# Sketched attention and a feed-forward block on one core: attention of the next batch placed among the feed-forward steps by a list scheduler, query sketches repeated by DMA

## Chip, core and metric

The kernel runs on one core of a Trainium2 chip. The metric is the device time of one execution in microseconds (us), as the median of several. The profiler's "span" is a little shorter than that time (by 1.75 us in the profiled run of the changed kernel). An execution is called slow when it is over 1.5% above the fastest one of the same kernel. Medians below are of all executions of a run; ratios and differences use the fast ones.

In profile lines, PE is TensorE's matmul work, PEld its weight loads, DVE is VectorE, ACT is ScalarE, POOL is GpSimd. SPq is the queue of SyncE, which issues most DMAs. L235 means line 235 of that kernel's own file, so the same line number in two kernels is not the same statement.

## The reference

There are 4 batches, 4 heads, 1088 tokens and a head size of 32. Each query and key is projected with two small 8x32 matrices. The products of the two sketches form 64 features, and attention becomes two small products with a division per token and head. The result (4352 tokens of 128) goes through a feed-forward block with a squared ReLU.

```python
def _attn_ref(q, k, v, S1, S2):              # q, k, v: (4, 4, 1088, 32); S1, S2: (8, 32)
    def phi(x):
        a = np.einsum('rd,bhsd->bhsr', S1, x)
        b = np.einsum('rd,bhsd->bhsr', S2, x)
        return np.einsum('bhsi,bhsj->bhsij', a, b).reshape(*x.shape[:-1], r * r)
    q_p, k_p = (phi(q), phi(k))
    kv = np.einsum('bhsf,bhsd->bhfd', k_p, v)
    z = np.sum(k_p, axis=2)
    num = np.einsum('bhsf,bhfd->bhsd', q_p, kv)
    den = np.einsum('bhsf,bhf->bhs', q_p, z)[..., None] + 1e-06
    return (num / den).astype(np.float32)

def _moe_ref(x, w_in, w_out):                # (4352, 128), (128, 2048), (2048, 128)
    h = x @ w_in
    r = np.maximum(h, 0.0)
    g = r * r
    return (g @ w_out).astype(np.float32)
```

The features of all queries need each sketch number next to each of eight others, so something has to repeat them. And a batch's feed-forward work needs only that batch's attention, so attention of a later batch can run beside it.

## The kernel before

Attention of all four batches comes first. The numerator is computed with the 32 outputs of a head on partitions and tokens along the free dimension, so the denominator of 512 tokens is one row on a single partition:

```python
            for hh in range(G):
                ...
                    nc.tensor.matmul(nd_ps[:, :C], kvz_sb[:, hh, :], qpT_all[:, hh, c0 : c0 + C],
                                     start=True, stop=True)
                    rec = den_pool.tile([1, NDC], F32, tag="rec")
                    nc.vector.reciprocal(rec[:, :C], nd_ps[D : D + 1, :C])          # L235
                    recb = den_pool.tile([D, NDC], F32, tag="recb")
                    nc.gpsimd.partition_broadcast(recb[:, :C], rec[:, :C])
                    nc.vector.tensor_mul(xT[h * D : (h + 1) * D, ...], nd_ps[:D, :C], recb[:, :C])
```

Then the feed-forward stage takes 512 tokens at a time, in 16 steps of 128 hidden units, two steps in flight:

```python
            for ct in range(C_TILES):
                hT = hT_psum_pool.tile([128, R_TILE], F32, tag="hT")
                nc.tensor.matmul(hT[:, :R], w_in_sb[:, ct, :], xT[:, r0 : r0 + R], start=True, stop=True)
                tmp = tmp_pool.tile([128, R_TILE], BF16, tag="tmp")
                nc.scalar.activation(tmp[:, :R], hT[:, :R], mybir.ActivationFunctionType.Relu)   # L270
                gT = gT_pool.tile([128, R_TILE], BF16, tag="gT")
                nc.vector.tensor_mul(gT[:, :R], tmp[:, :R], tmp[:, :R])                          # L274
                op = out_ps0 if ct % 2 == 0 else out_ps1
                nc.tensor.matmul(op[:, :R], w_out_sb[:, ct, :], gT[:, :R], ...)
```

The whole kernel:

Of the kernel before, what the change touches and what calls it, by code (L numbers as in the profile page):

```python
# [10 lines left out]
F32 = mybir.dt.float32  # L12
F32R = mybir.dt.float32r
BF16 = mybir.dt.bfloat16


def _mk_p2(nc, pool, a_sb, b_rep, P, r, F, tag, eng=None):
    p_out = pool.tile([128, 2 * F], F32, tag=tag, name=tag)
    (eng or nc.vector).tensor_tensor(  # L19
        out=p_out[:P].rearrange("p (hh i j) -> p hh i j", hh=2, i=r),  # L20
        in0=a_sb[:P, :, None].rearrange("p (hh i) j -> p hh i j", hh=2).to_broadcast(
            [P, 2, r, r]
        ),
        in1=b_rep[:P].rearrange("p (hh i j) -> p hh i j", hh=2, i=r),
        op=mybir.AluOpType.mult,
    )
    return p_out


def _mk_p(nc, pool, a_sb, b_rep, P, r, F, tag):  # L30
    p_out = pool.tile([128, F], F32, tag=tag, name=tag)
    nc.vector.tensor_tensor(
        out=p_out[:P].rearrange("p (i j) -> p i j", i=r),
        in0=a_sb[:P, :, None].to_broadcast([P, r, r]),
        in1=b_rep[:P].rearrange("p (i j) -> p i j", i=r),
        op=mybir.AluOpType.mult,
    )
    return p_out
# [3 lines left out]
def kernel(  # L42
# [11 lines left out]
    nc = tc.nc  # L54
    B, H, S, D = q.shape
    r = S1.shape[0]
    F = r * r
    d_model = moe_w_in.shape[0]
    d_ff = moe_w_in.shape[1]
    N_TOK = B * S  # L60
    assert d_model == H * D
    C_TILES = d_ff // 128
    G = 128 // D
    n_stiles = (S + 127) // 128

    consts = ctx.enter_context(tc.tile_pool(name="consts", bufs=1))

    S1Tf = consts.tile([D, r], F32)
    S2Tf = consts.tile([D, r], F32)
    nc.sync.dma_start(out=S1Tf, in_=S1.rearrange("r d -> d r"))  # L70
    nc.sync.dma_start(out=S2Tf, in_=S2.rearrange("r d -> d r"))
    S12Eb = consts.tile([128, G * r + G * F], F32)
    nc.gpsimd.memset(S12Eb, 0.0)
    for g in range(G):
        nc.vector.tensor_copy(
            S12Eb[g * D : (g + 1) * D, g * r : (g + 1) * r], S1Tf
        )
        nc.vector.tensor_copy(
            out=S12Eb[
                g * D : (g + 1) * D, G * r + g * F : G * r + (g + 1) * F  # L80
            ].rearrange("d (i j) -> d i j", i=r),
            in_=S2Tf[:, None, :].to_broadcast([D, r, r]),
        )

    ident = consts.tile([128, 128], F32)
    make_identity(nc, ident)
    xT = consts.tile([d_model, N_TOK], BF16)

    w_in_sb = consts.tile([128, C_TILES, 128], BF16)
    nc.gpsimd.dma_start(  # L90
        out=w_in_sb, in_=moe_w_in.rearrange("d (ct c) -> d ct c", c=128)
    )
    w_out_sb = consts.tile([128, C_TILES, 128], BF16)
    nc.gpsimd.dma_start(
        out=w_out_sb, in_=moe_w_out.rearrange("(ct c) d -> c ct d", c=128)
    )

    with (
        tc.tile_pool(name="qkT", bufs=2) as qkT_pool,
        tc.tile_pool(name="qkin", bufs=3) as qkin_pool,  # L100
        tc.tile_pool(name="vp", bufs=2) as v_pool,
        tc.tile_pool(name="proj", bufs=3) as proj_pool,
        tc.tile_pool(name="kp", bufs=3) as kp_pool,
        tc.tile_pool(name="qpT", bufs=2) as qpT_pool,
        tc.tile_pool(name="kvzsb", bufs=2) as kvz_pool,
        tc.tile_pool(name="den", bufs=3) as den_pool,
        tc.tile_pool(name="ps_a", bufs=2, space=bass.MemoryType.PSUM) as ps_a,
        tc.tile_pool(name="ps_t", bufs=2, space=bass.MemoryType.PSUM) as ps_t,
        tc.tile_pool(name="ps_kvz", bufs=2, space=bass.MemoryType.PSUM) as ps_kvz,
        tc.tile_pool(name="ps_nd", bufs=2, space=bass.MemoryType.PSUM) as ps_nd,  # L110
    ):
        bh = [(b, h) for b in range(B) for h in range(H)]
        for g in range(len(bh) // G):
            heads = bh[g * G : (g + 1) * G]
            b0 = heads[0][0]
            assert all(bb == b0 for bb, _ in heads)
            h0 = heads[0][1]

            qab_all_a = qkT_pool.tile([128, n_stiles, G * r], F32, tag="qab_a")
            qab_all_b = qkT_pool.tile([128, n_stiles, G * F], F32, tag="qab_b")  # L120
            kvz_ps = ps_kvz.tile([128, G * (D + 1)], F32, tag="kvz")
            for ti in range(n_stiles):
                s0 = ti * 128
                P = min(128, S - s0)
                q4 = qkin_pool.tile([128, 128], F32, tag="q4")
                k4 = qkin_pool.tile([128, 128], F32, tag="k4")
                nc.sync.dma_start(
                    out=q4[:P].rearrange("p (g d) -> p g d", d=D),
                    in_=q[b0, h0 : h0 + G, s0 : s0 + P, :].rearrange(
                        "g p d -> p g d"  # L130
                    ),
# [192 lines left out]
```

## Time and profile before

| | before |
|---|---|
| time, median of 3 | 368.46 us (368.08 to 369.57) |
| span of the profile | 366.2 us |
| attention ends, feed-forward starts | about 280 us |

The first lines of the profile page of the kernel before give busy time per engine, then the busy share in tenths in 40 equal slices of the span. PEclk is TensorE's granted clock in tenths of full speed. The last line shown is the chain of waits that ended last, split by line of code:

```profile
...
PE 262.6 (72%) x848; PEld 116.2 (32%) x850; DVE 272.6 (74%) x543; ACT 131.6 (36%) x386; POOL 38.7 (11%) x93
...
DVE  1146878995597899558879964898997888888874
...
PEclk9999555556965555596555559955555999999998
...
DVE rec L235 30%; PE nd_ps L227 9%; ACT tmp L270 6%; PE qab_ps L144 5%; PE kvz_ps L180 5%; PE kab_ps L164 5%; DVE gT L274 4%; PE hT L262 3%; POOL recb L237 3%; DVE xT L238 3%; PE qpT_ps L214 3%; DVE qpT_all L216 2%; PE qT_ps L140 2%; DVE qp
...
```

VectorE is busy 74% and TensorE 72%, but neither is the bound everywhere. The chain of waits shows the one-row reciprocal first, with 30% of the span. The clock row shows half speed through most of attention.

The groups of instructions by shape (count, busy us, mean ns of one, idle before and its causes):

```profile
...
L235 DVE RECIPROCAL rec<-nd_ps 1x512 f32<-1x512 f32 x32 | 105.5, 3324 | 12.4 <-PE nd_ps L227 12.4
L274 DVE TENSOR_TENSOR gT<-tmp 128x512 bf16<-128x512 bf16 x128 | 53.6, 422 | 15.5 <-ACT tmp L270 12.0 <-PE out_ps_2114 L276 0.3 <-PE out_ps_2577 L276 0.3
...
L235 DVE RECIPROCAL rec<-nd_ps 1x64 f32<-1x64 f32 x16 | 8.8, 549 | 0.5
...
```

```profile
...
L270 ACT ACTIVATE tmp<-hT 128x512 bf16<-128x512 f32 x128 | 72.4, 598 | 36.9 <-DVE gT L274 32.0 <-PE hT L262 1.6 <-PE ot_ps L290 1.1
...
```

A reciprocal of 512 numbers on one partition takes 3324 ns, 114 us for all 48. With 64 elements it takes 549 ns, so its cost follows the elements along the free dimension, and 127 partitions do nothing. A square of a full 128x512 tile costs 422 ns.

Busy time of each engine by stretch: two stretches of attention, and 9 us of the feed-forward stage:

```profile
...
100.00:200.00 100.00, 67.45 (x179) 30.29 (x180) 79.85 (x133) 17.89 (x84) 13.39 (x29) 0.58 0.13 21
245.00:280.00 35.00, 18.85 (x33) 3.67 (x33) 31.25 (x31) 3.79 (x7) 7.08 (x11) 0.50 0.00 0
300.00:309.00 9.00, 8.71 (x34) 3.19 (x33) 7.49 (x20) 8.72 (x16) 0.00 (x0) 1.00 0.07 22
...
```

Columns after the stretch: its length, busy us of PE, PEld, DVE, ACT, POOL, then granted clock, DMA share and GB/s. In attention the clock is 0.58 and 0.50. In the feed-forward stage ScalarE is full (8.72 of 9 us), at clock 1.00. TensorE's 8.71 us is as high, but the ends of matmuls are modelled in the profile, so this is no sign that it is at its peak.

### The profile page before, as it was taken

To read this page: it belongs to the slowest core of one execution; us is meant where nothing else is said; L and a number is where in the kernel's file an instruction comes from. 1 tells how busy PE (TensorE), PEld (TensorE's weight loads), DVE (VectorE), ACT (ScalarE), POOL (GpSimd) and SP (SyncE) were. 2 spreads that over 40 slices of the span, in tenths; PEclk is the share of its full clock that TensorE was granted. 3 is DMA by queue.
4 is the path that set the end of the run, shared out by engine and by line. 5 is a ranking of instruction groups with operands and counts; after the bars stand their busy time and mean duration, and the time that the engine had idled before them with its cause. 6 is when DMAs were issued, how large, how long until landed. Compare 5 with 4: busy or idle time off the path is not lost.

```text
span 366.2 us, 3606 instructions
## 1 busy us (share of the span) xinstructions
PE 262.6 (72%) x848; PEld 116.2 (32%) x850; DVE 272.6 (74%) x543; ACT 131.6 (36%) x386; POOL 38.7 (11%) x93
## 2 busy tenths in 40 slices
PE   0698365786836688593678659476654999999995
PEld 0474122335512233461223246221111333333332
DVE  1146878995597899558879964898997888888874
ACT  1144110001421100142110014241112999999984
POOL 1200011111001112101102210001211000000000
PEclk9999555556965555596555559955555999999998
DMA  7864001102400101150020122000000100100001
GB/s 108 86 100 64 2 15 21 20 10 35 78 7 13 24 12 16 29 85 7 0 34 9 19 32 35 0 0 0 0 0 2 30 30 29 30 23 21 18 26 44
DMA packets 61620, 10.19 MB, mean 28 GB/s; under 512 B 57120, under 2 KB 61472, under 8 KB 61600
## 3 DMA queue, kind: packets, MB, share of 16 engines
q1 hardware_dynamic: 59392, 8.92, 14.2%
q0 software_dynamic: 2208, 1.05, 2.3%
q8 instruction: 7, 0.11, 0.1%
q14 instruction: 13, 0.11, 0.1%
HBM read 8.78 MB, written 2.23 MB: 30 GB/s over the span
## 4 chain that ended last, share of the span: by engine, by line
DVE 42%; PE 37%; ACT 9%; issue 5%; POOL 3%; POOLq 0%; ACTq 0%; DVEq 0%
DVE rec L235 30%; PE nd_ps L227 9%; ACT tmp L270 6%; PE qab_ps L144 5%; PE kvz_ps L180 5%; PE kab_ps L164 5%; DVE gT L274 4%; PE hT L262 3%; POOL recb L237 3%; DVE xT L238 3%; PE qpT_ps L214 3%; DVE qpT_all L216 2%; PE qT_ps L140 2%; DVE qp L19 1%; DVE osb L292 1%
## 5 line engine op out<-in xcount | busy, mean ns | idle before, releaser
L235 DVE RECIPROCAL rec<-nd_ps 1x512 f32<-1x512 f32 (+1 forms) x48 | 114.3, 2399 | 12.9 <-PE nd_ps L227 12.4
L270 ACT ACTIVATE tmp<-hT 128x512 bf16<-128x512 f32 (+1 forms) x144 | 77.8, 574 | 38.4 <-DVE gT L274 32.8
L227 PE MATMUL nd_ps<-qpT_all,kvz_sb 64*33 64x512 f32 (+1 forms) x96 | 62.3, 773 | 40.2 <-DVE xT L238 39.5
L274 DVE TENSOR_TENSOR gT<-tmp 128x512 bf16<-128x512 bf16 (+1 forms) x144 | 57.8, 408 | 16.8 <-ACT tmp L270 13.2
L262 PE MATMUL hT<-xT,w_in_sb 128*128 128x512 bf16 (+1 forms) x143 | 54.5, 389 | 2.3 <-ACT tmp L270 0.6
L237 POOL PARTITION_BROADCAST recb<-rec x48 | 31.9, 664 | 152.8 <-DVE rec L235 152.8
L168 ACT COPY ka_sb<-kab_ps 128x32 f32<-128x32 f32 (+1 forms) x36 | 6.7, 185 | 104.7 <-PE kab_ps L164 104.7
L214 PE MATMUL qpT_ps<-ident,qp 128*128 128x128 f32 (+1 forms) x72 | 22.4, 368 | 24.4 <-DVE qp L19 17.3
L19 DVE TENSOR_TENSOR kp<-ka_sb,kab_ps 128x128 f32<-128x128 f32 (+1 forms) x72 | 18.2, 283 | 23.7 <-ACT ka_sb L168 23.0
L180 PE MATMUL kvz_ps<-vpad,kp 128*128 128x66 f32 (+1 forms) x144 | 28.1, 323 | 7.2 <-issue 6.2
L144 PE MATMUL qab_ps<-S12Eb,qT_sb 128*128 128x288 f32 (+1 forms) x72 | 32.8, 548 | 0.4
L164 PE MATMUL kab_ps<-S12Eb,kT_sb 128*128 128x288 f32 (+1 forms) x72 | 32.6, 543 | 0.0
L227 PEld LDWEIGHTS nd_ps<-qpT_all,kvz_sb 64*33 64x33 f32 x96 | 10.3, 143 | 70.1 <-issue 57.3
L180 PEld LDWEIGHTS kvz_ps<-vpad,kp 128*128 128x128 f32 (+1 forms) x144 | 23.6, 230 | 21.4 <-issue 19.3
L215 ACT COPY qpT_all<-qpT_ps 64x128 f32<-64x128 f32 (+1 forms) x72 | 16.2, 254 | 39.2 <-PE qpT_ps L214 38.7
L238 DVE TENSOR_TENSOR xT<-nd_ps,recb 32x512 bf16<-32x512 f32 (+1 forms) x48 | 24.9, 525 | 7.1 <-POOL recb L237 6.5
L19 DVE TENSOR_TENSOR qp<-qab_all_a,qab_all_b 128x128 f32<-128x128 f32 (+1 forms) x72 | 20.5, 299 | 9.7 <-ACT qab_all_b L148 5.0
L214 PEld LDWEIGHTS qpT_ps<-ident,qp 128*128 128x128 f32 (+1 forms) x72 | 10.3, 163 | 46.4 <-issue 30.7
L262 PEld LDWEIGHTS <-w_in_sb 128*128 128x128 bf16 x144 | 14.2, 100 | 29.6 <-issue 24.3
L276 PEld LDWEIGHTS <-w_out_sb 128*128 128x128 bf16 x144 | 13.8, 98 | 26.4 <-issue 15.8
L216 DVE COPY qpT_all<-qpT_ps 64x128 f32<-64x128 f32 (+1 forms) x72 | 18.6, 283 | 2.6 <-ACT qpT_all L215 1.9
L152 DVE COPY kT_sb<-kT_ps 128x128 f32<-128x128 f32 (+1 forms) x36 | 10.1, 280 | 13.6 <-PE kT_ps L150 13.4
(202 smaller groups left out, 199.0 us busy)
## 6 DMA issues: line engine op xcount, KB each, us to landing
out_dram<-osb SPq DMA_DIRECT2D x34, 64.0 KB, 1.6
vpad<-in_v_dram SPq DMA_DIRECT2D x32, 64.0 KB, 2.3
w_in_sb<-in_moe_w_in_dram POOLq DMA_DIRECT2D x1, 512.0 KB, 5.6
w_out_sb<-in_moe_w_out_dram POOLq DMA_DIRECT2D x1, 512.0 KB, 7.8
vpad<-in_v_dram SPq DMA_DIRECT2D x4, 32.0 KB, 2.2
q_121<-in_q_dram SPq DMA_DIRECT2D x1, 64.0 KB, 5.6
k_122<-in_k_dram SPq DMA_DIRECT2D x1, 64.0 KB, 5.4
q_150<-in_q_dram SPq DMA_DIRECT2D x1, 64.0 KB, 5.2
```

Of the source, the lines that this page charges most:

```text
L19: (eng or nc.vector).tensor_tensor(out=p_out[:P].rearrange("p (hh i j) -> p hh i j", hh=2, i=r), in0=a_sb[:P, :, None].rearrange("p (hh i) ...
L144: nc.tensor.matmul(qab_ps[:P], qT_sb[:, :P], S12Eb, start=True, stop=True)
L164: nc.tensor.matmul(kab_ps[:P], kT_sb[:, :P], S12Eb, start=True, stop=True)
L180: nc.tensor.matmul(kvz_ps[:, hh * (D + 1) : (hh + 2) * (D + 1)], kp[:P, :], vpad[:P, hh : hh + 2, :].rearrange("p g d -> p (g d)"), start= ...
L214: nc.tensor.transpose(qpT_ps[:, :P], qp[:P], ident[:P, :P])
L227: nc.tensor.matmul(nd_ps[:, :C], kvz_sb[:, hh, :], qpT_all[:, hh, c0 : c0 + C], start=True, stop=True,)
L235: nc.vector.reciprocal(rec[:, :C], nd_ps[D : D + 1, :C])
L237: nc.gpsimd.partition_broadcast(recb[:, :C], rec[:, :C])
L238: nc.vector.tensor_mul(xT[h * D : (h + 1) * D, b0 * S + c0 : b0 * S + c0 + C], nd_ps[:D, :C], recb[:, :C],)
L262: nc.tensor.matmul(hT[:, :R], w_in_sb[:, ct, :], xT[:, r0 : r0 + R], start=True, stop=True,)
L270: nc.scalar.activation(tmp[:, :R], hT[:, :R], mybir.ActivationFunctionType.Relu)
L274: nc.vector.tensor_mul(gT[:, :R], tmp[:, :R], tmp[:, :R])
```

## The change

The kernel is rebuilt. Its intent is to have no one-partition work, fewer and larger instructions, and attention of batches 1 to 3 hidden among the 68 feed-forward steps.

1. Tokens lie on partitions in the numerator, so a reciprocal works on 128x12.
2. A feed-forward step is 1024 columns wide, and its ReLU can run on ScalarE or VectorE.
3. The sketches of batch 0's queries are repeated by TensorE with a replicated weight matrix. For batches 1 to 3 they are repeated by eight DMAs a batch (`Ar` from `qs` in SBUF, `Br` from a bounce `bd` in DRAM), and GpSimd forms the products.
4. All operations go into a graph. A list scheduler, given a duration and a latency for each operation, fixes the order of every engine's queue when the kernel is built. Engines then execute strictly in that order.

The core of the diff (long parts cut). The scheduler picks, among operations that could start almost at once, the one of the best priority:

```diff
...
+                best = None
+                for e, (busy, lat) in o.alts.items():
+                    t = max(eng_free.get(e, 0.0), t_slot)
+                    for d in o.deps:
+                        t = max(t, d.end + (SEM if d.eng != e else 0.0))
+                    if e in o.port:
+                        t = max(t, port_free)
+                    if best is None or t + lat < best[0]:
+                        best = (t + lat, t, e, busy, lat)
+                cands.append((best[1], o, best))
+            assert cands, "no operation can start: " + ", ".join(o.name for o in ready[:20])
+            t0 = min(c[0] for c in cands)
+            _, o, (_, t, e, busy, lat) = min(
+                (c for c in cands if c[0] <= t0 + LOOK), key=lambda c: (c[1].pri, c[0]))
...
```

An operation's entry is (time for which its engine is held, time until its result is there), in us. The repeats, and the GpSimd products that need them, have these:

```diff
...
+            reps = []
+            for pr in range(2):
+                for hp in range(2):
+                    def f_rb(e, pr=pr, hp=hp):
+                        p0 = 16 * pr + 8 * hp
+                        nc.sync.dma_start(
+                            out=Br[i][64 * hp : 64 * hp + 64, pr, :],
+                            in_=bd[i][None, p0 : p0 + 8, :].to_broadcast([R, 8, S]))
+                    reps.append(add(f"rb{b}.{pr}.{hp}", {"SP": (0.5, 4.0)}, f_rb, o_bw + prev(b, "qp"), vt(4)))
+                for ch in range(2):
+                    def f_ra(e, ch=ch, pr=pr):
+                        p0 = 64 * ch + 16 * pr
+                        nc.sync.dma_start(
+                            out=Ar[i][:, pr, HS * ch : HS * ch + HS],
+                            in_=qs[i][p0 : p0 + 16, None, :].to_broadcast([16, R, HS]))
+                    reps.append(add(f"ra{b}.{ch}.{pr}", {"SP": (0.5, 4.0)}, f_ra, o_qe + prev(b, "qp"), vt(4)))
...
+                    def f_qp(e, pr=pr, c0=c0, n=n):
+                        en = nc.gpsimd if e == "POOL" else nc.vector
+                        sl = slice(c0, c0 + n)
+                        en.tensor_tensor(out=qp[i][:, pr, sl], in0=Ar[i][:, pr, sl], in1=Br[i][:, pr, sl], op=ALU.mult)
+                    o = add(f"qp{b}.{g}.{pr}", {"POOL": pool(n)}, f_qp, reps[4 * pr : 4 * pr + 4] + prev(b, "num"),
+                            vt(6 + g), port=("POOL", "DVE"))
+                    mine("qp", o)
...
```

Here a repeat, with `(0.5, 4.0)`, holds its queue 0.5 us and lands 4.0 us after its start, and a product of n columns has the two times of `pool(n)`. The numerator with tokens on partitions, the division, and one feed-forward step:

```diff
...
-            NDC = 512
-            for hh in range(G):
-                h = h0 + hh
-                c0 = 0
-                while c0 < S:
-                    C = min(NDC, S - c0)
-                    nd_ps = ps_nd.tile([D + 1, NDC], F32, tag="nd")
-                    nc.tensor.matmul(
-                        nd_ps[:, :C],
-                        kvz_sb[:, hh, :],
-                        qpT_all[:, hh, c0 : c0 + C],
-                        start=True,
-                        stop=True,
-                    )
-                    rec = den_pool.tile([1, NDC], F32, tag="rec")
-                    nc.vector.reciprocal(rec[:, :C], nd_ps[D : D + 1, :C])
-                    recb = den_pool.tile([D, NDC], F32, tag="recb")
-                    nc.gpsimd.partition_broadcast(recb[:, :C], rec[:, :C])
-                    nc.vector.tensor_mul(
-                        xT[h * D : (h + 1) * D, b0 * S + c0 : b0 * S + c0 + C],
-                        nd_ps[:D, :C],
-                        recb[:, :C],
-                    )
-                    c0 += C
...
+                for x in range(3):
+                    for pr in range(2):
+                        for cc in range(4):
+                            c = 4 * (3 * g + x) + cc
+                            if c >= C:
+                                c -= 2
+                            nc.tensor.matmul(
+                                t[32 * cc : 32 * cc + 32, x, 2 * pr : 2 * pr + 2, :],
+                                qp[i][:, pr, 32 * c : 32 * c + 32],
+                                kvz[i][:, pr], start=True, stop=True)
...
+            def f_den(e, nb=nb, i2=i2):
+                t = a_t[nb.slot][:, 0:396].rearrange("p (m d) -> p m d", d=33)
+                nc.vector.tensor_scalar_add(den[i2], t[:, :, D], eps)
+                nc.vector.reciprocal(rec[i2], den[i2])
+                nc.vector.tensor_tensor(
+                    out=xs[i2].rearrange("p x (h d) -> p (x h) d", d=D), in0=t[:, :, 0:D],
+                    in1=rec[i2][:, :, None].to_broadcast([128, 12, D]), op=ALU.mult)
+            o_mx = add(f"mx{b}.{g}", {"DVE": dve(384, fix=0.55)}, f_den,
...
+            o1 = add(f"m1.{n}.{m}", {"PE": pe(W * N / 2400)}, f_m1, deps + [o_win], p, alloc=[hb])
+            def f_r(e, hb=hb, rb=rb):
+                if e == "ACT":
+                    nc.scalar.activation(r_t[rb.slot], h_t[hb.slot], ACTF.Relu)
+                else:
+                    nc.vector.tensor_scalar_max(r_t[rb.slot], h_t[hb.slot], 0.0)
+            o2 = add(f"r.{n}.{m}", {"ACT": act(W * N), "DVE": dve(W * N)}, f_r, [o1], p - 0.5, alloc=[rb], uses=[hb])
+            def f_g(e, rb=rb, gb=gb):
+                nc.vector.tensor_tensor(out=g_t[gb.slot], in0=r_t[rb.slot], in1=r_t[rb.slot], op=ALU.mult)
+            o3 = add(f"g.{n}.{m}", {"DVE": dve(W * N, 0.53e-3)}, f_g, [o2], p - 0.6, alloc=[gb], uses=[rb],
+                     port=("POOL", "DVE"))
...
```

And the priorities: a batch's attention ranks a little before the feed-forward steps that precede its own.

```diff
...
+    first = [0, 2, 4, 6]
+    for b in range(B):
+        if b == 0:
+            vt = lambda d: -40 + d
+        else:
+            s1 = 8 * first[b] - 3.0
+            s0 = s1 - 15.0
+            vt = lambda d, s0=s0, s1=s1: s0 + (s1 - s0) * d / 12.0
+        attention(b, vt)
+    for n, n0, N in chunks:
+        ffn(n, n0, N, 8.0 * n)
+    order = G.run()
+    global LAST_GRAPH
+    LAST_GRAPH = G
+    with tc.manual_schedule():
+        for o in order:
+            o.fn(o.eng)
```

## The prediction

> **What bounds the kernel now.** Span 366 us, two stages. Attention runs to about 280 us. There the chain of waits is 30% reciprocal (chain by line): 32 one-partition reciprocals of 512 elements take 3324 ns each, 16 of 64 take 549 ns (groups by shape), 114 us in all, and TensorE waits on them. The granted clock is 0.56 to 0.62 until 245 us (busy time by stretch). The feed-forward stage then is ScalarE-bound: 8.58 of every 9 us busy at clock 1.0; a 128x512 ReLU takes 598 ns, a square 422 ns. The stages hardly overlap.
>
> **What the change does.**
> - Removes the one-partition reciprocals: tokens lie on partitions, so 48 become 12 of 12 elements (estimate from 3324 and 549 ns: 0.23 us each). Also gone: 48 partition broadcasts, query-product transposes with 144 copies, output transposes on TensorE.
> - ReLU and square work on 1024 columns. Fitting the 256 and 512 forms: ReLU on ScalarE 1.03 us, square 0.70 us; from the PSUM reads on VectorE (283 ns at 128, 687 ns at 512), ReLU there 1.22 us. The built order has 55 ReLUs on ScalarE, 13 on VectorE.
> - Moves attention of batches 1 to 3 among the 68 feed-forward steps; only batch 0 is exposed.
> - Adds eight repeating DMAs and two bounce writes per later batch, and 18 products on GpSimd.
>
> **Cost after (estimates from those durations and the built order).**
> VectorE: squares 47.5, ReLU 16, key products 11, query products of batch 0 2.7, 32x32 transposes 12.5, normalising 11, output transposes 6, small 2: 108 us, of which 19 before the first square. ScalarE: ReLU 57, copies 14: 71 us. TensorE: 272 matmuls of 512 columns at 216 ns ("TensorE: Matmul & The Clock Gate", Back-to-back issue gap; the trace gives two per 600 ns step at clock 1.0, so it agrees only as a bound) is 59 us, plus 25 to 40 us of small fp32 matmuls. So VectorE bounds the interleaved stage.
>
> Sum: 28 us until the first square (loads 7 to 10, from 150 to 180 GB/s seen at the start; then batch 0's chain), plus 90 us of VectorE work, 16 us of stalls (late repeat DMAs: 2.2 MB a batch at such rates is over 10 us, and queues are in fixed order; latencies between engines), 3.5 us of tail, 2.3 us between span and time: **140 us**. Range 125 to 160 (8 in 10). Chances: faster 0.99, same 0.005, slower 0.005.
>
> Contention is in the stalls: "SBUF — State Buffer", Who interferes with whom, says a VectorE instruction with two SBUF inputs and a GpSimd one that reads SBUF exclude each other. Squares and GpSimd's products are such a pair; no run here shows it yet. I give it 5 us.
>
> **What would show it right.** VectorE the busiest, 75 to 85%; ScalarE near 50%; reciprocals under 4 us; feed-forward beginning by 25 to 32 us; clock near 1.0 afterwards; one wait on DMA per later batch before the query product.
>
> **What would make it wrong.** Repeat DMAs far slower than 10 us a batch, so the fixed order stops all engines (160+). The clock staying half: 4 matmuls of 512 columns a step would cost 1.7 us and TensorE bound at 155+. Small fp32 matmuls (24 per numerator group) not overlapping across column groups: several us each. Squares stretched by GpSimd. On the other side, quicker loads and few stalls: 122.

## The result

| | before | after |
|---|---|---|
| time, median | 369.01 us (4 runs, 368.08 to 369.87) | 148.70 us (146.35, 147.06 fast; 150.35, 153.02 slow) |
| ratio of fast runs | | 0.3971 (95% interval 0.3941 to 0.4002) |
| span, granted clock | 366.2 us, 0.716 | 144.6 us, 0.934 |

A ratio here is the mean time of one kernel's fast runs over that of the other's fast runs of the same rounds, so it is not quite the ratio of the quoted medians. The prediction was 140 us with a range of 125 to 160.

The same lines of the page of the kernel after:

```profile
...
PE 106.7 (74%) x1507; PEld 58.8 (41%) x1524; DVE 101.9 (70%) x192; ACT 67.7 (47%) x90; POOL 30.2 (21%) x48
...
PE   0008999799970496998999999995018898999850
...
DVE  1219789898991038969999998693002999998960
...
PEclk9999999999999559999999999999555999999997
...
DVE 31%; PE 23%; SPq 15%; DMA 14%; issue 8%; POOL 1%; ACT 1%; POOLq 1%; DVEq 0%; ACTq 0%
DVE g L543 13%; SPq L451 7%; DMA S_sb<-in_S_dram 6%; PE o L550 6%; SPq L444 5%; PE h L531 5%; DMA Br<-bd 4%; DMA out_dram<-osb 4%; DVE r L539 4%; PE a L483 4%; SPq L566 3%; PE h L396 3%; DVE osb L557 3%; DVE xs L495 2%; PE a L359 2%
...
```

VectorE fell from 272.6 to 101.9 us, TensorE from 262.6 to 106.7 us. The reader should see two gaps that go through the PE and DVE rows at once: around slices 13 to 15 and 28 to 30 (a slice is 3.6 us). The clock falls to half in both. In the chain, 29% of the span is no compute: 15% in SyncE's queue and 14% in DMAs.

The groups of the kernel after, by shape:

```profile
...
L543 DVE TENSOR_TENSOR g<-r 128x1024 bf16<-128x1024 bf16 x68 | 45.2, 706 | 1.8 <-ACT r L537 1.1 <-PE a L483 0.6
L539 DVE TENSOR_SCALAR r<-h 128x1024 bf16<-128x1024 f32 x13 | 15.8, 1218 | 3.6 <-PE h L531 3.6
...
L494 DVE RECIPROCAL rec<-den 128x12 f32<-128x12 f32 x12 | 2.7, 228 | 0.4
...
```

```profile
...
L537 ACT ACTIVATE r<-h 128x1024 bf16<-128x1024 f32 x55 | 54.6, 1023 | 21.7 <-PE h L531 16.2 <-DVE g L543 4.2 <-PE o L550 1.0
...
```

Twelve reciprocals take 2.7 us in all instead of 114.3. ReLU and square have the durations that were predicted (next section but one). The stretches of the kernel after, with the same columns as before:

```profile
...
30.00:40.00 10.00, 9.75 (x141) 5.56 (x136) 9.41 (x17) 6.68 (x10) 1.73 (x2) 1.00 0.85 148
...
44.00:57.00 13.00, 6.86 (x190) 4.91 (x191) 4.23 (x11) 2.27 (x4) 5.54 (x6) 0.74 0.74 152
...
99.50:110.00 10.50, 2.36 (x51) 1.41 (x50) 0.17 (x1) 0.72 (x1) 3.60 (x4) 0.61 0.45 130
...
```

I call 44 to 57 us hole A and 99.5 to 110 us hole B. VectorE idles 8.8 us in A (13.00 less 4.23) and 10.3 us in B (10.50 less 0.17), 19 us together. What it waits for is the list of VectorE's waits (us in total, times, longest):

```profile
...
DVE den L493 <- PE a L483: 20.6, 4, 10.6
...
```

The denominator waits for the numerator's matmuls: 20.6 us in four waits. Those matmuls wait for GpSimd's products, as the group of their line (`L483`) on the page shows:

```profile
...
L483 PE MATMUL a<-kvz,qp 128*32 128x66 f32 x576 | 13.8, 252 | 16.5 <-POOL qp L464 15.0
...
```

Follow one step further back, to SyncE's queue (start, us, what is issued, how many). First hole A, then hole B:

```profile
...
29.87 0.80 SPq L435 DMA_DIRECT2D bd<-qs  x2
30.71 6.53 SPq L451 DMA_DIRECT2D Ar<-qs  x4
37.35 3.94 SPq L444 DMA_DIRECT2D Br<-bd  x4
...
```

```profile
...
86.65 0.79 SPq L435 DMA_DIRECT2D bd<-qs  x2
87.53 0.60 SPq L451 DMA_DIRECT2D Ar<-qs  x1
88.23 4.01 SPq L566 DMA_DIRECT2D out_dram<-osb  x4
92.34 3.23 SPq L451 DMA_DIRECT2D Ar<-qs  x3
95.61 4.46 SPq L444 DMA_DIRECT2D Br<-bd  x4
...
```

And GpSimd's products in both:

```profile
...
45.26 0.99 POOL L464 TENSOR_TENSOR qp<-Ar,Br 128x384 f32<-128x384 f32 x1 [5.52 <-DMA Br<-bd]
47.91 4.54 POOL L464 TENSOR_TENSOR qp<-Ar,Br 128x384 f32<-128x384 f32 x5 [1.67 <-issue]
```

```profile
...
104.10 0.99 POOL L464 TENSOR_TENSOR qp<-Ar,Br 128x384 f32<-128x384 f32 x1 [34.36 <-DMA out_dram<-osb]
107.39 3.72 POOL L464 TENSOR_TENSOR qp<-Ar,Br 128x384 f32<-128x384 f32 x4 [2.30 <-DMA out_dram<-osb]
```

For hole A the queue takes 10.5 us to issue the eight repeats of batch 1 (6.53 + 3.94), and GpSimd makes one product at 45.26 and goes on only at 47.91, 17.2 us after the first repeat began to issue. (The profile names no cause for that second wait, "issue". By the diff the first product needs one half of the repeats and the second the other half. Between the two TensorE ran only 8 of the 48 records of a group's numerator matmuls. So I read that wait as the landing of the other half.) The scheduler believed in 7.5 us: seven issues of 0.5 and a latency of 4.0. It placed the numerators of batch 1 in TensorE's queue for that time, and TensorE, which executes in order, stood still with feed-forward work behind them. The excess of 9.7 us is close to the 8.8 us that VectorE idles in hole A. A single repeat can issue in about the scheduler's 0.5 us: over all 24 the shortest took 0.57 us, but the longest 2.36. Hole B has the same shape, with one addition: four output stores (4.01 us, from 88.23) stand in SyncE's queue between the first repeat and the other seven. The wait at 104.10 is put down to an output DMA. The product itself reads only `Ar` and `Br`, whose last repeats were issued by 100.07, so I read it as the repeats' landing.

That reading is the theory: **holes A and B come from repeats that land some 10 us later than the scheduler's numbers say.** It has rivals. The prefetch loads of later batches may slow the repeats down. Starting the repeats earlier may be enough, whatever the numbers. VectorE's total work may be what binds, and the holes only slack. Or the late start of TensorE may set the time.

### The profile page after: what moved, and what is told of

Read it like the earlier page. It is cut to its first block, busy times and chain, and to the rows that moved or that the text cites. A ratio compares the mean times of both kernels' runs of the same rounds, so it can differ in the third digit from the quotient of the medians.

```text
span 144.6 us, 3697 instructions
## 1 busy us (share of the span) xinstructions
PE 106.7 (74%) x1507; PEld 58.8 (41%) x1524; DVE 101.9 (70%) x192; ACT 67.7 (47%) x90; POOL 30.2 (21%) x48
## 4 chain that ended last, share of the span: by engine, by line
DVE 31%; PE 23%; SPq 15%; DMA 14%; issue 8%; POOL 1%; ACT 1%; POOLq 1%; DVEq 0%; ACTq 0%
DVE g L543 13%; SPq L451 7%; DMA S_sb<-in_S_dram 6%; PE o L550 6%; SPq L444 5%; PE h L531 5%; DMA Br<-bd 4%; DMA out_dram<-osb 4%; DVE r L539 4%; PE a L483 4%; SPq L566 3%; PE h L396 3%; DVE osb L557 3%; DVE xs L495 2%; PE a L359 2%
## 5 line engine op out<-in xcount | busy, mean ns | idle before, releaser
L537 ACT ACTIVATE r<-h 128x1024 bf16<-128x1024 f32 x55 | 54.6, 1023 | 21.7 <-PE h L531 16.2
L543 DVE TENSOR_TENSOR g<-r 128x1024 bf16<-128x1024 bf16 x68 | 45.2, 706 | 1.8 <-ACT r L537 1.1
L531 PE MATMUL h<-xT,w_in 128*128 128x512 bf16 (+1 forms) x135 | 38.8, 373 | 1.7 <-DVE r L539 0.4
L550 PE MATMUL o<-g,w_out 128*128 128x512 bf16 (+1 forms) x136 | 37.7, 367 | 2.5 <-DVE g L543 1.3
L464 POOL TENSOR_TENSOR qp<-Ar,Br 128x384 f32<-128x384 f32 (+1 forms) x18 | 17.5, 998 | 54.7 <-DMA out_dram<-osb 36.7
L483 PE MATMUL a<-kvz,qp 128*32 128x66 f32 x576 | 13.8, 252 | 16.5 <-POOL qp L464 15.0
L531 PEld LDWEIGHTS <-w_in 128*128 128x128 bf16 x144 | 13.5, 98 | 18.1 <-issue 5.0
L550 PEld LDWEIGHTS <-w_out 128*128 128x128 bf16 x144 | 12.8, 97 | 16.9 <-issue 7.2
L483 PEld LDWEIGHTS a<-kvz,qp 128*32 128x32 f32 x576 | 11.2, 128 | 20.8 <-POOL qp L464 17.8
L539 DVE TENSOR_SCALAR r<-h 128x1024 bf16<-128x1024 f32 x13 | 15.8, 1218 | 3.6 <-PE h L531 3.6
L493 DVE TENSOR_SCALAR den<-a 128x12 f32<-128x12 f32 x12 | 2.0, 164 | 20.6 <-PE a L483 20.6
```

The source lines that it names most:

```text
L464: en.tensor_tensor(out=qp[i][:, pr, sl], in0=Ar[i][:, pr, sl], in1=Br[i][:, pr, sl], op=ALU.mult)
L483: nc.tensor.matmul(t[32 * cc : 32 * cc + 32, x, 2 * pr : 2 * pr + 2, :], qp[i][:, pr, 32 * c : 32 * c + 32], kvz[i][:, pr], start=True, st ...
L531: nc.tensor.matmul(h_t[hb.slot][:, N * w : N * w + N], w_in[:, 128 * ct : 128 * ct + 128], xT[:, n0 : n0 + N], start=True, stop=True)
L537: nc.scalar.activation(r_t[rb.slot], h_t[hb.slot], ACTF.Relu)
L539: nc.vector.tensor_scalar_max(r_t[rb.slot], h_t[hb.slot], 0.0)
L543: nc.vector.tensor_tensor(out=g_t[gb.slot], in0=r_t[rb.slot], in1=r_t[rb.slot], op=ALU.mult)
```

## The experiments

Twelve kernels ran. Each was compared with the kernel before in the same rounds. Runs 1 to 4 shared one chip, as did 5 to 8, 9 and 10, and 11 and 12. "The changed kernel" is the kernel after.

### 1. The changed kernel again

No edit. It checks that the holes are there again, on the chip of runs 2 to 4.

> The changed kernel once more, unchanged, as the control of this call. Fast runs 145 to 148.5 us. The same two holes in VectorE's work should lie at the same places in the trace: about 9 us between 44 and 57 us and about 10 us between 99.5 and 110 us from the start. If the holes move or vanish from run to run, they are chance and not the order of the queues.

Measured: 148.35 us (147.04 and 147.40 fast; 149.3 and 151.65 slow), ratio 0.3986 (0.3955 to 0.4017). VectorE was busy 10.25 of the 20 us from 40 to 60, and 0.86 of the 10 us from 100 to 110. The holes repeat.

### 2. No repeating DMAs: TensorE repeats the sketches of all batches

```diff
-        if b == 0:
+        if True:
             for g in range(3):                  # batch 0's way, for every batch
...
-                o_ac = add(f"qa{b}.{g}", {"ACT": act(2 * n)}, f_ac, [ms[0]], vt(3 + g), uses=[hA])
+                o_ac = add(f"qa{b}.{g}", {"ACT": act(2 * n)}, f_ac, [ms[0]] + prev(b, "qp"), vt(3 + g), uses=[hA])
...                                              # and the like for the product, as buffers are reused
```

> The query sketches of all batches are repeated by TensorE as batch 0's are; no repeating DMAs, no bounce, no GpSimd products. Theory (the holes are late repeating DMAs met by fixed queues): both holes vanish. VectorE's work rises from 101.9 by 3 x 2.7 to 110 us, of which 89 after the first square; 30 us to the first square, 89 at 93% busy, 6.5 tail, 1.7 to the time: 134 us (130 to 138). Rival (VectorE is the limit and the holes only move): the extra 8 us show, 150 us or more. Rival (squares and GpSimd products exclude each other and that costs much): the mean square falls from 706 to about 650 ns.

Measured: 136.35 us (135.89 to 136.54, all fast), ratio 0.3690 (0.3670 to 0.3710). Busy time by stretch, where the holes were:

```profile
...
40.00:50.00 10.00, 9.57 (x137) 4.90 (x136) 9.47 (x19) 7.72 (x10) 0.00 (x0) 1.00 0.08 14
...
100.00:110.00 10.00, 9.44 (x41) 3.74 (x40) 9.63 (x16) 6.84 (x9) 0.00 (x0) 1.00 0.16 27
...
```

Both holes are gone at clock 1.00. A square takes 688 ns in the mean instead of 706, so contention with GpSimd was not what made them. VectorE now does more (110.5 us busy instead of 101.9, 82% of the span) and the kernel is still faster. The repeating DMAs cost more in order than they saved in work. This alone doesn't say whether their lateness or something else about them did it; the next run does.

### 3. Only the scheduler's numbers for the repeats

The same instructions as the changed kernel. Only the order that is computed from these numbers changes. 1.3 us is the measured mean time to issue one, and 8.0 makes seven issues and a latency 17.1 us, against the 17.2 measured.

```diff
-  reps.append(add(f"rb{b}.{pr}.{hp}", {"SP": (0.5, 4.0)}, f_rb, o_bw + prev(b, "qp"), vt(4)))
+  reps.append(add(f"rb{b}.{pr}.{hp}", {"SP": (1.3, 8.0)}, f_rb, o_bw + prev(b, "qp"), vt(4)))
...
-  reps.append(add(f"ra{b}.{ch}.{pr}", {"SP": (0.5, 4.0)}, f_ra, o_qe + prev(b, "qp"), vt(4)))
+  reps.append(add(f"ra{b}.{ch}.{pr}", {"SP": (1.3, 8.0)}, f_ra, o_qe + prev(b, "qp"), vt(4)))
```

> Only the numbers that the order is computed from are changed: a repeating DMA takes 1.3 us to issue and 8 us to land instead of 0.5 and 4. Same instructions, same bytes, same engines. The built order moves the numerators of batch 1 from after 8 second matmul steps to after 14, and the query sketch of batch 3 from step 30 to step 14. Theory (the order believes in DMAs that are too quick): both holes shrink to under 3 us each, 130 us (127 to 136). Rival (the repeats load the DMA engines or GpSimd's port so that all else slows down): within 2% of the control, 144 to 149 us, with waits in other places.

Measured: 134.08 us (132.98 to 135.29), ratio 0.3620 (0.3593 to 0.3648). The profiled run was the slow one of the four. Where the holes were:

```profile
...
40.00:50.00 10.00, 10.00 (x140) 5.25 (x137) 9.83 (x20) 7.75 (x12) 4.65 (x5) 1.00 0.68 174
...
100.00:110.00 10.00, 8.89 (x42) 3.62 (x41) 9.54 (x16) 6.55 (x8) 0.00 (x0) 1.00 0.15 26
```

The repeats themselves are about as slow as before: batch 1's first product starts 13.6 us after its first repeat is issued (33.50 to 47.08), against 14.6 us in the changed kernel (30.71 to 45.26). What changed is the work that the other engines do meanwhile. The wait of the denominator on the numerators (20.6 us in the changed kernel) is no longer among the longest: VectorE's longest waits are 5.3 us in eight pieces on ReLU's input and 4.6 us for the sketch matrices at the start. Two pairs of numbers take 13.5 us off (fast runs of both on one chip, 147.2 to 133.7 in the mean) with no other change. That is the strongest support for the theory.

One cost became visible. The group line of the squares:

```profile
...
L543 DVE TENSOR_TENSOR g<-r 128x1024 bf16<-128x1024 bf16 x68 | 50.8, 787 | 2.5 <-ACT r L537 2.2
...
```

A square now takes 787 ns in the mean, against 706 in the changed kernel and 688 in run 2, where GpSimd does no such products. Run 11 takes this up.

### 4. Loads of batches 2 and 3 held back behind the repeats

A rival says that the prefetch loads fill the DMA engines while the repeats run.

```diff
+        hold = hist.get((b - 1, "bw"), []) if b > 1 else []
+        lp = vt(0) - 30 if b < 2 else vt_prev[0](4) + 1
...
-        o_k = add(f"ldk{b}", {"SP": (0.6, 3.4)}, ld(kin[i], k, 0, C), prev(b, "tk"), vt(0) - 30)
+        o_k = add(f"ldk{b}", {"SP": (0.6, 3.4)}, ld(kin[i], k, 0, C), prev(b, "tk") + hold, lp)
...                                              # the same for q and v
```

> The loads of batches 2 and 3 are issued after the repeats of the batch before, not ahead of them. Order of the other engines is about the same. Rival (the first hole is prefetch that stands ahead of the repeats in the same queue): the first GpSimd product of batch 1 starts at 41 us or earlier instead of 45.3, and the hole before 50 us shrinks by 4 us or more; the time falls by 4 to 6 us. Theory (the repeats themselves take some 10 us to issue and 5 more to land): the product starts no more than 1.5 us earlier, the time moves by less than 2 us, because batch 2's eight repeats took 9.6 us to issue with no loads about and batch 1's 10.5.

Measured: 167.14 us (165.53 to 168.09), ratio 0.4511 (0.4476 to 0.4545). The repeats of batch 1 took 9.6 us to issue and its first product started at 44.49, only 0.8 us before the changed kernel's 45.26. So prefetch ahead of the repeats is not what makes them slow. The second product started later, at 49.66 instead of 47.91, with the held-back loads now issued right behind the repeats; what such traffic costs their landing is not shown. The 13% that the kernel lost I had not expected. The wait list shows it:

```profile
...
DVE kT L317 <- DMA kin<-in_k_dram: 31.0, 3, 14.0
...
```

Held back this far, the loads come after VectorE needs them. A new instance of the same lesson: SyncE's one queue carries loads, repeats and stores, and what is put behind the repeats is late by their issue time.

### 5. Repeats of half the bytes

If the repeats' time is in their bytes, bf16 sketches halve it. The order stays as in the changed kernel.

```diff
-    qs = [T(f"qs{i}", [128, HS]) for i in range(NB)]
+    qs = [T(f"qs{i}", [128, HS], BF16) for i in range(NB)]
...                                              # Ar, Br and the bounce bd in the same way
```

> The changed kernel in its own order; only the repeated sketches (qs, bounce, Ar, Br) are bf16, so each repeating DMA moves half the bytes in the same number of pieces; results are a little less exact. If the landing of the repeats is set by bytes: eight repeats issue in about 5 us instead of 10, the first product of batch 1 starts near 38 us instead of 45, both holes nearly close, 132 to 138 us. If it is set by a fixed cost per DMA or per piece: the product starts no more than 2 us earlier, and the time stays within 3 us of the control's 147.

Measured: 128.11 us (127.80 to 128.69), ratio 0.3479 (0.3464 to 0.3494), with a **wrong result** (relative error 0.726). Denominators have either sign here, so a small one may magnify rounding. No run tests that. In the numpy reference, rounding only these sketches to bf16 changes the output by a relative 0.41, so rounding can cause an error of this order. SyncE's queue:

```profile
...
31.97 3.10 SPq L451 DMA_DIRECT2D Ar<-qs  x4
35.18 2.62 SPq L444 DMA_DIRECT2D Br<-bd  x4
...
```

Issuing the eight repeats took 5.7 us instead of 10.5, and the first product of batch 1 started at 39.82 instead of 45.26. The holes all but close: VectorE is busy 9.25 of the 10 us from 40 to 50, and it still loses 3.8 us from 90 to 100. So the lateness follows the bytes. It is not that each issue is cheaper: the shortest takes 0.57 us with either size, and only the longer ones shrink (the longest from 2.36 to 0.98 us). Nor are bytes enough, as a key load of 544 KB issues in 0.35 to 0.77 us in the changed kernel. What the longer issues wait for stays open, and no run issued the repeats from a second queue or in another shape. With an unchanged order, the mean of the fast runs falls by 18.5 us (146.7 to 128.2), about as much as the two holes cost VectorE, and below the 132 to 138 us that I expected. One reason why it is also faster than run 3 is in the traces: only 2 squares overlap a GpSimd product here, and 16 in run 3 (run 11 says what that costs).

### 6. True numbers and an earlier start

TensorE begins only at 11.48 us in the changed kernel, because the sketch matrices come by eight small loads, the last of which lands at 10.15. Here each is loaded once and copied to the other partitions by VectorE.

```diff
-            for h in range(H):
-                nc.scalar.dma_start(out=S_sb[32 * h + off : 32 * h + off + R, :], in_=S)
+            nc.scalar.dma_start(out=S_sb[off : off + R, :], in_=S)
...                                              # plus three VectorE copies, and the edit of run 3
```

> e2_true_latency, and S1 and S2 loaded once each (2 DMAs instead of 8) and spread to the other partitions by three VectorE copies. In the trace of the changed kernel the last small load lands at 10.2 us and TensorE begins at 11.5, though k has been there since 5.1. Theory: the start is bound by those eight loads, the last two of which were issued only after 5 us because each waits for the semaphore of an earlier load: TensorE begins at 7 to 8 us and the time falls by 3 to 4 us from e2's 133 to 134: 130 us (129 to 132). Rival (q at about 10 us bounds batch 0 anyway): under 1 us gained.

Measured: 133.56 us (132.03 to 136.39, 6 runs; profile slow), ratio 0.3616 (0.3597 to 0.3634): no gain that can be told from run 3. TensorE did begin at 8.00 us. VectorE's longest wait is now:

```profile
...
DVE kT L316 <- DMA kin<-in_k_dram: 5.5, 2, 4.1
...
```

VectorE waits for the keys twice, 5.5 us in all, against once, 4.0 us, in run 3. (Both profiles are of slow executions.) That explains only a part. The first square starts at 29.39 us, 3.4 us before run 3's 32.77, and by 33 us VectorE has done about 2.5 us more work. By 110 us it is 1.1 us ahead, about the 1.0 us by which its work in this run is longer (109.2 us against 108.3). So the lead was won and lost again among the feed-forward steps. My expectation of 130 us failed, and no single wait that I can show explains the loss.

### 7. No overlap of attention and feed-forward

Run 2 with every feed-forward step made to wait for all of attention, to measure what the interleaving is worth.

```diff
-        deps = [o for lo, hi, o in x_ops if lo < n0 + N and hi > n0]
+        deps = [o for lo, hi, o in x_ops]
```

> e1_pe_repeat with every feed-forward step made to wait for all four batches' attention, so no interleaving. If interleaving is a main part of the gain: the attention of batches 1 to 3 is exposed, some 14 us each at batch 0's pace of 18 us with overlap, feed-forward alone 68 steps at about 1.0 us: 30 + 40 + 68 + 8 = 146 us, that is 10 us over e1. If little overlap existed, the time is within 2 us of e1's 136.4. A rival for the gain, that the stages were bound by the same VectorE work anyway, would say 138 to 141.

Measured: 142.44 us (142.36 to 144.26), ratio 0.3878 (0.3849 to 0.3907), 6.6 us more than run 2 in the mean of the fast runs, where I expected 10. The first square starts at 65.7 us. So the interleaving, which looked like the heart of the change, is worth about 5% here, and a kernel without any interleaving beats the changed kernel (fast runs 146.35 to 147.4 us). VectorE has nearly the same work either way (114.4 us against 110.5), so overlap could only fill its waits.

### 8. The kernel before with nothing but the wide reciprocal

```diff
-  nc.tensor.matmul(nd_ps[:, :C], kvz_sb[:, hh, :], qpT_all[:, hh, c0 : c0 + C], ...)
-  nc.vector.reciprocal(rec[:, :C], nd_ps[D : D + 1, :C])
-  nc.gpsimd.partition_broadcast(recb[:, :C], rec[:, :C])
+  for hh in range(G):
+      nc.tensor.matmul(nd_ps[:P, hh, :], qpT_all[:, hh, s0 : s0 + P], kvz_sb[:, hh, :], ...)
+  nc.vector.reciprocal(rec[:P], nd_ps[:P, :, D])
...                                              # then the product, and a transpose on TensorE
```

> The kernel before, with one part of the change alone: the numerator and denominator computed with tokens on partitions, so that the 48 one-partition reciprocals and 48 partition broadcasts become 36 reciprocals of 4 columns, with a transpose back. If the chain of reciprocals (114 us in the profile of before) is the largest single part of the gain: 369 falls by 90 to 125 us, to 245 to 280 us. If TensorE and the copies are just behind it: by less than 60 us.

Measured: 294.24 us (292.28 to 294.85), ratio 0.7977 (0.7936 to 0.8017). 75 us, less than I expected, although the reciprocals fell to 6.5 us. The first line of its page and two of its groups:

```profile
...
PE 262.5 (90%) x1076; PEld 162.2 (55%) x1078; DVE 150.4 (51%) x519; ACT 141.0 (48%) x422; POOL 6.5 (2%) x45
...
```

```profile
...
L225 PE MATMUL nd_ps<-kvz_sb,qpT_all 64*128 64x33 f32 x256 | 58.0, 385 | 0.0
...
L225 PEld LDWEIGHTS nd_ps<-kvz_sb,qpT_all 64*128 64x128 f32 x256 | 53.6, 307 | 8.1 <-issue 5.7 <-PE hT L264 1.1 <-ACT kvz_sb L190 0.9
...
```

TensorE is now busy 90% of the span and has 69% of the chain that ended last, 20% in these matmuls alone. The layout turns 48 wide numerator matmuls into many small ones, each with a 128-column weight load of 307 ns in front. In the whole rebuild the numerator (`L483`) has its weights and its matmuls on four column groups at once: 24 matmuls of a group take 0.90 us at full clock (48 records from 24.42 us), so this second bound doesn't arise there.

### 9. Run 2 with every ReLU on ScalarE

The rival "VectorE's work binds" says that taking 14 ReLUs off VectorE (17 us) should gain most of that.

```diff
-  o2 = add(f"r.{n}.{m}", {"ACT": act(W * N), "DVE": dve(W * N)}, f_r, [o1], ...)
+  o2 = add(f"r.{n}.{m}", {"ACT": act(W * N)}, f_r, [o1], ...)
```

> e1_pe_repeat with all 68 ReLUs on ScalarE (14 of them were on VectorE at 1.22 us each). VectorE's work falls from 110.5 to 93.5 us, ScalarE's rises from 70.7 to about 85. If VectorE is what bounds the interleaved stage, as the prediction said: 136.4 falls by 6 to 11 us, to 125 to 130 us, and ScalarE becomes nearly as busy. Rival (the two PSUM buffers for the hidden layer, not VectorE, set the pace, so that one engine alone emptying them is slower): 136 us or more.

Measured: 133.81 us (133.63 to 136.05), ratio 0.3627 (0.3610 to 0.3644). VectorE fell from 110.5 to 98.8 us and the time by 2.5 us only. By stretch, and VectorE's longest wait:

```profile
...
100.00:110.00 10.00, 9.50 (x41) 3.85 (x40) 7.99 (x13) 9.80 (x11) 0.00 (x0) 1.00 0.20 34
...
```

```profile
...
DVE g L543 <- ACT r L537: 12.0, 34, 1.1
...
```

ScalarE is now full late in the kernel. There ScalarE is busy 9.80 of 10 us, TensorE 9.50 and VectorE 7.99, so taking work off VectorE gains little. I expected 6 to 11 us, and that was wrong.

### 10. Run 9 with the earlier start

The edits of runs 9 and 6 together.

> e10 with the two small loads of e6 in place of eight. In e6 TensorE began 3.9 us earlier, but the time did not fall, because VectorE's fixed order then waited for batch 1's k and q, which had not landed. If that is the reason, the same is seen here: within 1.5 us of e10. If e6's gain was hidden only by e2's other waits (GpSimd's products), 2 to 4 us under e10.

Measured: 134.97 us (133.30 to 135.46), ratio 0.3646 (0.3626 to 0.3667). No gain, as expected after run 6.

### 11. Run 3 with each GpSimd product done twice

It tests the cost that run 3 showed: "SBUF — State Buffer", Who interferes with whom, in the Trainium skill, says that a VectorE instruction with two SBUF inputs contends with a GpSimd one that reads SBUF. If so, the squares must lengthen when GpSimd's share doubles.

```diff
-  en.tensor_tensor(out=qp[i][:, pr, sl], in0=Ar[i][:, pr, sl], in1=Br[i][:, pr, sl], op=ALU.mult)
+  for _ in range(2): en.tensor_tensor(out=qp[i][:, pr, sl], in0=Ar[i][:, pr, sl], in1=Br[i][:, pr, sl], op=ALU.mult)
```

> e2_true_latency with each of the 18 GpSimd products done twice over, all else and all orders the same. In e2 the mean square took 787 ns, against 680 in e7_no_overlap, which has no GpSimd products, and the 128x384 product 1247 ns against 999 in the changed kernel, where it fell into VectorE's holes. If squares and products exclude each other: the mean square rises to 850 to 900 ns, VectorE's busy time by 4 to 8 us, the product stays near 1.2 us each. If the squares of e2 are slow for another reason (DMA traffic, the scheduler's order): 787 ns stays within 15 ns. The time may rise by 5 to 15 us in any case, as the products also stand before the numerators.

Measured: 140.15 us (138.12 to 140.55; the fast ones are 138.12 and 139.77). The squares again:

```profile
...
L543 DVE TENSOR_TENSOR g<-r 128x1024 bf16<-128x1024 bf16 x68 | 55.3, 854 | 1.5 <-ACT r L537 1.2
...
```

Mean square: 680 ns in run 7 and 688 in run 2 (no GpSimd product), 706 in the changed kernel, 787 in run 3, 854 here. The trace agrees with the skill. Taken one by one, squares that overlap no GpSimd instruction take 679 to 681 ns in the mean in the changed kernel and in runs 2, 3, 5, 7 and 11. Those that overlap a product take 1102 ns in run 3 (16 of 68) and 1243 ns here (20 of 68). So the longer mean is not a matter of run 3's slow profile. The scheduler knew of it too: `port=("POOL", "DVE")` in the diff keeps such a pair apart in its own plan, but the plan's times were not the chip's. The changed kernel hardly paid because its products ran in the holes, when VectorE had no squares to do (3 squares overlap a product). Filling the holes brought the two together, at a price of about 7 us of VectorE time in run 3 (68 squares times 787 less 688).

### 12. The scheduler's wrong numbers kept, batches 2 and 3 eight steps earlier in priority

If starting earlier is enough, hole B should shrink without any true number.

```diff
-            s1 = 8 * first[b] - 3.0
+            s1 = 8 * first[b] - 3.0 - (8.0 if b > 1 else 0.0)
```

> The changed kernel with its own, too short, DMA numbers; only the priority of the attention of batches 2 and 3 is raised by 8 feed-forward steps. In the built order batch 3's query sketch goes from step 30 to 23 and its numerators from 41 to 35, while batch 1's numerators stay after step 8. Theory: the second hole (10 us at 100 to 110) is batch 3 begun too late and closes; the first hole (9 us at 44 to 57) stays: 136 to 140 us. Rival (one common cause, for instance DMA traffic, for both): both stay or both go.

Measured: 150.87 us (148.21 to 151.76; profile slow), ratio 0.4036 (0.3996 to 0.4075). My expectation of 136 to 140 us missed by about 9 us (fast runs 148.21 and 150.18). SyncE's queue around hole B:

```profile
...
82.39 1.88 SPq L435 DMA_DIRECT2D bd<-qs  x2
84.79 3.78 SPq L566 DMA_DIRECT2D out_dram<-osb  x8
88.67 5.58 SPq L451 DMA_DIRECT2D Ar<-qs  x4
94.31 3.87 SPq L444 DMA_DIRECT2D Br<-bd  x4
...
```

The bounce writes of batch 3 started 4.3 us earlier (82.39 against 86.65). But eight output stores now stood in front of the repeats, the last repeats left the queue at 98.18 instead of 100.07, and the first product came at 102.41 instead of 104.10. VectorE is busy 0.95 of the 10 us from 100 to 110. By the built order batch 3's query sketch moved from step 30 to 23 and its numerators from 41 to 35. So the numerators moved ahead together with the sketch, and the distance between the two, which must cover the repeats, grew only from 11 to 12 steps. That is my reading of why nothing was gained. With true latencies (run 3) batch 1's numerators moved from step 8 to 14 and batch 3's sketch from 30 to 14.

### All runs

| run | median us | what it shows |
|---|---|---|
| changed kernel (again) | 148.7 (148.35) | two holes, 19 us of VectorE |
| 2 TensorE repeats | 136.35 | no repeating DMAs, no holes |
| 3 true numbers | 134.08 | order alone is worth 13.5 us |
| 4 loads held back | 167.14 | prefetch ahead not the cause; loads late |
| 5 half the bytes (wrong result) | 128.11 | lateness follows the bytes |
| 6 true numbers, earlier start | 133.56 | no gain; the lead at the start is lost later |
| 7 run 2 without overlap | 142.44 | overlap is worth 6.6 us |
| 8 before, wide reciprocal only | 294.24 | 75 us, then TensorE binds |
| 9 run 2, ReLU on ScalarE | 133.81 | ScalarE full late; VectorE alone does not bind |
| 10 run 9, earlier start | 134.97 | no further gain |
| 11 run 3, products twice | 140.15 | squares lengthen beside GpSimd's products |
| 12 priority only | 150.87 | an earlier priority alone gains nothing |

Runs 3, 6 and 9 give right results at about 134 us, 9% under the changed kernel. They can't be told apart here.

## Why the prediction was right, and where it was off

The predicted sum and the profile of the fast run of 146.35 us, term by term:

| term | predicted us | measured us |
|---|---|---|
| until the first square | 28 | 29.98 |
| VectorE work after it | 90 | 82.3 (busy from 29.98 to 139.36) |
| stalls | 16 | 27.1 (the same 109.4 us less 82.3) |
| tail after the last square | 3.5 | 5.2 |
| span to time | 2.3 | 1.75 |
| sum | 140 | 146.35 |

That the total came within 5% is partly luck: VectorE's work after the first square was put 7.7 us too high and the stalls 11.1 us too low, and the two errors cancel in part.

- **The removal was right.** Reciprocals fell to 2.7 us (predicted under 4), at 228 ns each (predicted 230). Run 8 shows that this step alone gives 75 us and then meets TensorE.
- **The durations of the wide forms held.** ReLU on ScalarE 1023 ns (1.03 us predicted), on VectorE 1218 ns (1.22), square 706 ns (0.70), all worked out from the two widths in the old trace.
- **"VectorE the busiest" did not hold as stated.** TensorE is busy 106.7 us (74%, with modelled ends) and VectorE 101.9 (70%). The prediction gave TensorE 84 to 99 us. Run 9 shows that VectorE does not bind alone: 11.7 us less work for it saved 2.5 us.
- **VectorE's total was 101.9 us, not 108.** The mean durations times counts of all groups add up to 112.5 us, 4% above the prediction, but the trace shows neighbours overlapping: 68 squares of 706 ns would be 48.0 us and are 45.2 us busy. A sum of durations overstates a pipelined engine somewhat.
- **The step that failed is the size of "16 us of stalls (late repeat DMAs ...)".** The mechanism named there is the right one: fixed queue order, repeats over 10 us a batch. The stalls measured 27 us, of which the holes A and B are 19. The prediction gave the repeats "over 10 us" and in hole A they took 17.2 from the first issue until GpSimd could go on with its second product. It did not compare that with the 4.0 us in the kernel's own graph, which was readable in the diff. Runs 2, 3 and 5 tie the excess to that number. The rest, about 8 us, is small waits. Run 2 has as many: VectorE is idle 7.6 of the 95 us from 30 to 125 there.
- **Contention of GpSimd and VectorE was given 5 us; the changed kernel paid about 1.8** (68 times 706 less 680). The mechanism exists (run 11), but the holes hid it.
- **VectorE at 70% and not 75 to 85%, and the clock.** Both follow largely from the holes: the granted clock is 1.00 between them (57 to 99.5 us), 0.51 from 48 to 54 us and 0.50 from 102 to 112. "TensorE: Matmul & The Clock Gate", What's actually happening, in the Trainium skill, says that the clock halves after an idle window of about 3.4 us. In the trace the clock halves at 47.1 us in hole A, 4.5 us after TensorE's stream of matmuls ended (42.56) and with only a burst of 0.3 us between, which fits. In hole B it halves at 101.7, only 1.9 us after the last matmul (99.86), so there less than such a window of full idleness was enough. "One wait on DMA per later batch" was right for batches 1 and 3. For batch 2 it was 1.3 us.
- **The clock of the kernel before was told too narrowly** (0.56 to 0.62 until 245 us). It is 0.73 in the first 100 us, 0.58 from 100 to 200 and 0.69 from 200 to 245. Nothing in the sum rested on it.

Where did 220 us go? The experiments give a ladder, whose steps are differences between whole kernels and not independent parts: 369 before, 294 with the wide reciprocal (run 8), 142 with all of the rebuild's forms but neither overlap nor repeating DMAs (run 7), 136 with overlap (run 2). The largest step, 152 us, is the wide forms: fewer and larger instructions, and small matmuls on column groups. TensorE falls from 262.5 to 116.2 us in it. No run takes that step apart further, so the split within it stays open. The repeating DMAs then took 11 us back (fast runs, 147.2 against 136.3), until the scheduler was told the truth about them.

## What to carry to other kernels

An order fixed when the kernel is built is only as good as its latencies, and a DMA's latency is the one most easily wrong: measure issue and landing in a trace and put those in, before moving priorities. In a queue that runs in order, one late DMA stops every engine whose next instruction depends on it, however much independent work stands behind. Ask of work moved to another engine what it excludes, since idle time may hide that cost until the idle time is gone.

## What the Trainium skill lacked or had wrong

- **"DMA: Bandwidth & Descriptors", Issuing engines are not separate DMA queues**, says that the time to initiate a DMA is usually small relative to the DMA itself. Here the issue of eight repeats of 272 KB held SyncE's queue for 10.5 of the 17.2 us until GpSimd's second product. Over all 24 repeats the shortest issue took 0.57 us and the longest 2.36, and batch 1's eight took 5.7 us with half the bytes, so most of that is probably not initiation but waiting, for what is not shown. The page has no rate for a DMA that repeats SBUF rows over partitions: 2.23 MB in 17.2 us is 130 GB/s.
- **"VectorE: DVE Perf Modes", First, the fixed hardware budget**, says that a reciprocal is an iterative divide with a repeat count of 8, and gives no time. Here it is 6.2 ns for each further element along the free dimension (3324 less 549 ns over 448), and 228 ns for 128x12.
- **"TensorE: Matmul & The Clock Gate", Back-to-back issue gap**, gives about 131 ns a matmul at N=512 for a sustained stream and about 216 ns for the isolated gap. In the changed kernel 163 of the 211 pairs of consecutive N=512 matmuls start 215 ns apart and none starts closer; in run 9 it is 159 of 209. That is the second figure, in a stream with weight loads between, and the first was never reached.
- **"SBUF — State Buffer", Who interferes with whom**, was right that the pair contends, and gives no cost for this pair. Here a 128x1024 square went from 680 ns to 787 in the mean with 18 GpSimd products beside 68 squares, and to 854 with 36. A square that overlaps a product took up to 1494 ns in run 3.
